# A fused attention read and MoE on one core: the whole program in another written order, some operations on other engines

## The chip, the cores and the metric

The kernel runs on one core of a Trainium2 chip. What counts is the device time of one execution in microseconds (us). The compute engines are TensorE (PE in the profile, its weight loads PEld), VectorE (DVE), ScalarE (ACT) and GpSimd (POOL); SyncE (SP) issues nearly all DMA transfers. About 0.5% of the time is what a measurement of this kernel can tell from no change.

## What is computed

Two stages, all in fp32. For each of 8 batches and 8 heads, x (512 by 64) reads from a state (32 by 64) and the state reads from x; the 544 rows of a batch, its heads side by side, are tokens of a feed-forward layer with squared ReLU:

```python
scores = scale * np.matmul(x, state.transpose(0, 1, 3, 2))
...
a /= a.sum(-1, keepdims=True) + 1e-09
xread = np.matmul(a, state)
scores2 = scale * np.matmul(state, x.transpose(0, 1, 3, 2))
...
sread = np.matmul(a2, x)
return np.concatenate([xread, sread], axis=2)
...
h = np.maximum(x @ w_in, 0.0)
return (h * h @ w_out).astype(np.float32)
```

There are 4352 tokens of 512 features, w_in is 512 by 2048 and w_out 2048 by 512. The weights come as 64-bit floats and are turned to fp32 on the chip (a *decode*: a clamp, an activation, a shift and an "or" of 32-bit words).

## The kernel before

**Precision.** TensorE multiplies in a rounded fp32 format. To keep fp32's accuracy, an operand is split in a rounded high part and the rest (hi and lo); a product takes three matmuls: hi hi, hi lo, lo hi. So behind nearly each tile there is a cast on ScalarE (hi) and a subtraction (lo), which a key puts on POOL or VectorE.

**Blocks.** The MoE's tokens come in nine blocks: 0 to 7 are the 512 read rows of a batch, 8 holds the 256 state rows of all batches. The read itself is not computed for blocks 0 to 7: the states are multiplied into w_in first (the tiles w2ps and w4ps), and the softmax's weights, transposed (k_hi, k_lo), are multiplied with that. For a block there are 16 pieces of the hidden layer. `hidden(blk, fc)` (tile ph) is 12 matmuls of 512 columns into one of two PSUM buffers, then ReLU and square on ScalarE or VectorE (r, ph), the cast g_hi and the subtraction g_lo, after which the buffer is free; `accumulate(blk, fc)` (tiles acc) is 12 matmuls more into four PSUM buffers. Blocks 0 and 1 break their sum off at pieces 4 and 8, keep it (first, part) and add it at the end. Blocks 5 to 7 are *fast*: two pieces of the hidden layer at a time go through seven products of sums of their quarters (steps `fast.blk.p.h`, products m1 to m7). Their operands are made by small sums and splits, f_sum, d_sum and e_sum (tiles s), p_lo, f_lo and b_lo (tiles a_g_lo and b_g_lo), each on VectorE or POOL by a key; the sums of w_out that they need are made in the steps `sums.p` (tiles v, sv, both, first).

**Order.** The program is cut in steps, each a Python generator. `PLAN` (from line 25) is a list of 2835 entries written out by hand; each entry advances the step of that name to its next yield, so PLAN sets the order in which instructions are issued. The string that would loosen it, `LOOSE_FROM = "never"`, is no entry of PLAN. Therefore the helper `InOrder` around each engine (lines 407 to 421) keeps every instruction in the written order on its engine, all 645 us long; since it makes the call, nearly each row of the profile stands on its line, 417:

```python
op = call(*args, **kw)
if self.held:
    self.tc.keep_in_program_order(op)
```

SP's queue of transfers is in written order as well. An instruction that waits for a tile from another engine holds up all that is written behind it on its own engine.

**Engines.** `SECOND` (from line 368) lists, by kind of operation, the keys that take the second of two engines: `pick(key, a, b)` gives b for a listed key; `evac(key)` copies out of PSUM on VectorE if listed, otherwise on ScalarE; `split(..., key)` subtracts on VectorE if listed, otherwise on POOL; `decode` clamps on POOL if listed, otherwise on VectorE. ROWS, which is not touched, names the small tiled products that are issued as one row.

**The start.** x of batches 0 and 1 is loaded in four pieces (xn), transposed by TensorE (px) and copied (xT); the states are transposed (pd) and copied (sD); `scores.0` (st) is copied (`keep_s`, tile e), transposed (pst), and softmax.0 makes k_hi and k_lo. w_in is decoded from wi_raw to wf; `direct_w2.0` makes its first product with the states (w2ps). 22 small matmuls of the identity (`warm`, tile pw) fill gaps. Then hidden.0.0 can begin.

**The end.** The last step, fast.7.7.1, has its products in the order m1, m4 and m3, m5 and m2, m7, m6, and `store_end` combines and writes the two last tiles.

Of the kernel before, what the change touches and what calls it, by code (L numbers as in the profile page):

```python
# [25 lines left out]
    ident warm.0 start.0 start.0 load.0.1 prep.0.0 warm.1 prep.0.0 warm.2 load_raw.0 load.0.1 load_states.0  # L26
        prep.0.1 load_states.0 load_states.0 prep.0.1 warm.3 decode_wi.0 neg_ident load_raw.1 warm.4 prep.0.0
        warm.5 start.1 warm.6 decode_wi.0 warm.7 prep.0.1 start.1 prep.0.0 load_wo.0 load.1.1 decode_wi.0
        decode_wi.0 states.0 warm.8 warm.9 prep.0.1 states.0 load_raw.2 decode_wi.0 scores.0 decode_wi.1 keep_s.0.1
        load.1.1 decode_wi.1 warm.10 keep_s.0.0 warm.11 prep.1.0 transposed_scores.0.1 decode_wi.1 prep_wo.0  # L30
        decode_wi.1 prep.1.0 transposed_scores.0.0 decode_wi.1 load_wo.1 direct_w2.0 softmax.0.1 direct_w2.0
        warm.12 softmax.0.1 direct_w2.0 softmax.0.1 warm.13 softmax.0.0 direct_w2.0 direct_w2.0 warm.14 softmax.0.0
        warm.15 direct_w2.0 softmax.0.0 warm.16 softmax.0.1 direct_w2.0 softmax.0.1 decode_wi.2 warm.17 second_w2.0
        softmax.0.0 softmax.0.0 prep_wo.1 prep_wo.0 prep_wo.0 warm.18 warm.19 second_w2.0 warm.20 second_w2.0
        warm.21 load_raw.3 prep.1.1 second_w2.0 second_w2.0 decode_wi.2 second_w2.0 prep.1.1 softmax.0.1 prep.1.1
        decode_wi.2 softmax.0.1 prep.1.0 load_wo.2 softmax.0.1 prep_wo.2 load_wo.8 decode_wi.2 prep.1.1 load_raw.4
        softmax.0.0 prep_wo.0 prep.1.0 load_wo.3 softmax.0.0 decode_wi.2 prep_wo.1 prep_wo.0 softmax.0.0 scores.1
        keep_s.1.0 decode_wi.3 load_states.2 keep_s.1.1 hidden.0.0 decode_wi.3 hidden.0.0 prep_wo.1 prep_wo.1
        hidden.0.0 decode_wi.3 prep_wo.0 hidden.0.0 transposed_scores.1.1 transposed_scores.1.0 decode_wi.4
        hidden.0.1 softmax.1.1 prep_wo.2 softmax.1.0 load_states.2 hidden.0.1 load_wo.4 softmax.1.1 prep_wo.3  # L40
        prep_wo.1 softmax.1.0 decode_wi.3 prep_wo.1 hidden.0.0 hidden.0.0 softmax.1.0 hidden.0.1 hidden.0.1
        accumulate.0.0 decode_wi.3 direct_w2.1 prep_wo.2 direct_w2.1 load_raw.5 accumulate.0.0 prep_wo.2
        direct_w2.1 direct_w2.1 direct_w2.1 decode_wi.4 direct_w2.1 direct_w2.1 softmax.1.1 hidden.0.1 load_wo.5
        second_w2.1 hidden.0.2 prep_wo.2 softmax.1.0 decode_wi.4 load_wo.7 hidden.0.1 accumulate.0.1 hidden.0.2
        hidden.0.2 decode_wi.4 softmax.1.0 load_raw.6 second_w2.1 second_w2.1 prep_wo.3 hidden.0.2 softmax.1.1
        hidden.0.3 softmax.1.0 accumulate.0.1 second_w2.1 decode_wi.4 prep_wo.2 hidden.0.3 softmax.1.0 exp_s.0.1
        hidden.0.2 hidden.0.2 softmax.1.1 second_w2.1 second_w2.1 load_wo.6 accumulate.0.2 hidden.0.3 exp_s.0.1
        prep_wo.3 softmax.1.1 decode_wi.5 decode_wi.5 prep_wo.3 softmax.1.1 softmax.1.0 hidden.0.3 load_states.2
        prep_wo.3 decode_wi.5 softmax.1.1 decode_wi.5 hidden.0.3 hidden.0.3 load_wo.11 decode_wi.5 prep_wo.4
# [1533 lines left out]
```

## Time and profile before

| | us |
|---|---|
| median of three runs | 644.88 (644.7 to 646.84) |
| the profiled execution | 646.96 |
| its span, first to last instruction | 645.1 |
| mean granted TensorE clock | 0.999 |

The profile is of one execution. A row of the timeline gives start, duration, engine, operation, the tile written and those read, and in brackets how long the engine had been idle before it and what released it. A row of the chain or of the waits has its columns named at the group. "x4" is the count of instructions taken together.

### The profile page before, as it was taken

How to read it: one execution, taken by the hardware profiler on the slowest of the kernel's cores; microseconds unless marked ns; L12 is line 12 of the kernel's file. 1: busy time of each engine (PE TensorE's matmuls, PEld its weight loads, DVE VectorE, ACT ScalarE, POOL GpSimd, SP SyncE). 2: the span in 40 equal slices, each digit the busy share in tenths (PEclk: the TensorE clock that was granted, in tenths of full speed). 3: DMA queues.
4: the chain of work that ended last, by engine and by line, in shares of the span. 5: the costliest groups of instructions: out<-in, count | busy, mean ns of one | idle time of the engine just before them, and what ended most of it. 6: DMA issues, size and time to landing. Idle time of an engine off the chain costs nothing.

```text
span 645.1 us, 12288 instructions
## 1 busy us (share of the span) xinstructions
PE 631.9 (98%) x4453; PEld 528.1 (82%) x4453; DVE 465.8 (72%) x927; ACT 394.7 (61%) x815; POOL 184.5 (29%) x172
## 2 busy tenths in 40 slices
PE   7999999999999999999999999999999999999996
PEld 6677787888777778777787788887999999999995
DVE  3999888675675688686958543579999866577637
ACT  3888667655654376655555542666877755565563
POOL 1665351201430124421023210223000344325451
PEclk9999999999999999999999999999999999999999
DMA  8888886989879889888977831421113332214202
GB/s 280 279 285 277 252 276 214 295 274 236 256 181 313 237 205 265 192 233 237 257 256 206 228 105 35 133 65 49 34 49 113 118 115 66 66 50 148 65 1 67
DMA packets 153132, 113.07 MB, mean 175 GB/s; under 512 B 93168, under 2 KB 126448, under 8 KB 153072
## 3 DMA queue, kind: packets, MB, share of 16 engines
q1 hardware_dynamic: 152784, 112.03, 59.5%
q8 instruction: 35, 0.57, 0.4%
q10 hardware_dynamic: 288, 0.26, 0.1%
q14 instruction: 25, 0.20, 0.1%
HBM read 72.94 MB, written 39.32 MB: 174 GB/s over the span
## 4 chain that ended last, share of the span: by engine, by line
PE 94%; DVE 2%; issue 1%; DMA 1%; ACT 1%; SPq 0%; POOLq 0%; POOL 0%; DVEq 0%; ACTq 0%
PE acc L417 37%; PE ph L417 30%; PE m L417 18%; PE w2ps L417 3%; PE w4ps L417 2%; PE pr L417 1%; PE st L417 1%; PE pw L417 1%; DMA xn<-in_x_dram 1%; PE px L417 1%; DVE g_lo L417 1%; DVE ph L417 0%; PE pst L417 0%; ACT r L417 0%; PE pa L417 0%
## 5 line engine op out<-in xcount | busy, mean ns | idle before, releaser
L417 PE MATMUL acc<-wo,g_hi 128*128 128x512 f32 x704 | 203.8, 393 | 0.0
L417 PE MATMUL ph<-k_hi,w 128*128 128x512 f32 x512 | 176.1, 392 | 0.4 <-DVE g_lo L417 0.3
L417 PEld LDWEIGHTS acc<-wo,g_hi 128*128 128x128 f32 x704 | 130.6, 188 | 32.6 <-issue 2.5
L417 ACT ACTIVATE r<-ph 128x512 f32<-128x512 f32 (+1 forms) x124 | 70.4, 569 | 97.8 <-PE ph L417 92.6
L417 PE MATMUL acc<-wo,g_lo 128*128 128x512 f32 x352 | 122.1, 391 | 0.0
L417 PEld LDWEIGHTS ph<-k_hi,w 128*128 128x128 f32 x512 | 96.2, 188 | 21.4 <-issue 1.2
L417 PE MATMUL ph<-k_lo,w 128*128 128x512 f32 x256 | 100.3, 392 | 0.0
L417 PEld LDWEIGHTS acc<-wo,g_lo 128*128 128x128 f32 x352 | 65.7, 188 | 14.7 <-DVE dec L417 0.4
L417 DVE TENSOR_TENSOR g_lo<-ph,g_hi 128x512 fp32r<-128x512 f32 (+1 forms) x95 | 60.4, 640 | 23.3 <-ACT g_hi L417 18.9
L417 DVE SCALAR_TENSOR_TENSOR ph<-ph,r 128x512 f32<-128x512 f32 (+1 forms) x48 | 31.1, 648 | 42.3 <-ACT r L417 42.1
L417 PEld LDWEIGHTS ph<-k_lo,w 128*128 128x128 f32 x256 | 48.2, 188 | 8.2
L417 POOL TENSOR_TENSOR w<-w_f,w 128x512 fp32r<-128x512 f32 x21 | 28.9, 1383 | 74.1 <-ACT w L417 37.9
L417 POOL TENSOR_TENSOR sp<-sp,m 128x512 f32<-128x512 f32 x25 | 26.6, 1067 | 72.3 <-DVE m L417 67.5
L417 ACT ACTIVATE g_hi<-r 128x512 fp32r<-128x512 f32 (+1 forms) x76 | 44.0, 582 | 4.9 <-PE acc L417 3.8
L417 POOL TENSOR_TENSOR wf<-wf,wf_hi 128x512 fp32r<-128x512 f32 x8 | 10.9, 1367 | 67.9 <-ACT wf_hi L417 67.9
L417 ACT ACTIVATE ph<-ph 128x512 f32<-128x512 f32 x40 | 23.5, 587 | 10.1 <-PE ph L417 8.6
L417 ACT CAST w<-w_f 128x512 fp32r<-128x512 f32 x40 | 24.2, 614 | 6.6 <-DMA w_f<-w_d 6.5
L417 POOL TENSOR_SCALAR dec<-wo_raw 128x512 f32<-128x512 f32 x10 | 20.5, 2051 | 13.3 <-DMA wo_raw<-in_moe_w_out_dram 13.1
L417 ACT ACTIVATE g<-r 128x512 f32<-128x512 f32 x35 | 21.8, 630 | 0.4
L417 DVE TENSOR_REDUCE m<-sp 128x16 f32<-128x512 f32 x28 | 18.7, 670 | 3.3 <-ACT sp L417 3.1
L417 POOL TENSOR_TENSOR s<-sf,s 128x512 fp32r<-128x512 f32 x6 | 7.8, 1292 | 43.3 <-ACT s L417 43.3
L417 ACT COPY w4o<-w4ps 128x512 f32<-128x512 f32 x16 | 9.1, 588 | 13.8 <-PE w4ps L417 9.7
(1072 smaller groups left out, 1309.6 us busy)
## 6 DMA issues: line engine op xcount, KB each, us to landing
w_f<-w_d SPq DMA_DIRECT2D x40, 256.0 KB, 4.0
wi_raw<-in_moe_w_in_dram SPq DMA_DIRECT2D x16, 512.0 KB, 5.1
wo_raw<-in_moe_w_out_dram SPq DMA_DIRECT2D x16, 512.0 KB, 5.7
xr<-in_x_dram SPq DMA_DIRECT2D x16, 512.0 KB, 5.5
wf<-win_f SPq DMA_DIRECT2D x16, 512.0 KB, 5.2
w_d<-w4o SPq DMA_DIRECT2D x32, 256.0 KB, 4.1
w<-w2a_d SPq DMA_DIRECT2D x16, 512.0 KB, 3.6
out_dram<-o SPq DMA_DIRECT2D x30, 256.0 KB, 3.0
```

The lines of the kernel that those rows point to most:

```text
L417: op = call(*args, **kw)
```

## The change

PLAN is written in another order, with the same 2835 entries, each as often as before; SECOND has other keys. No step, no instruction, no transfer and no buffer is added or taken away, and ROWS and all functions are as they were. On TensorE, 518 of 596 groups of matmuls keep their order among themselves; most others swap with a neighbour. 252 operations change their engine: 90 go from VectorE to POOL, 87 from POOL to VectorE, 39 from ScalarE to VectorE and 36 from VectorE to ScalarE. The first lines of PLAN, and some of SECOND:

```diff
 PLAN = """
-    ident warm.0 start.0 start.0 load.0.1 prep.0.0 warm.1 prep.0.0 warm.2 load_raw.0 load.0.1 load_states.0
-        prep.0.1 load_states.0 load_states.0 prep.0.1 warm.3 decode_wi.0 neg_ident load_raw.1 warm.4 prep.0.0
-        warm.5 start.1 warm.6 decode_wi.0 warm.7 prep.0.1 start.1 prep.0.0 load_wo.0 load.1.1 decode_wi.0
...
+    ident warm.0 warm.3 start.0 start.0 load.0.1 load.0.1 load_states.0 load_states.0 load_states.0 warm.18
+        load_raw.0 warm.21 warm.4 warm.2 warm.7 load_raw.1 start.1 start.1 prep.0.0 prep.0.0 prep.0.1 prep.0.0
+        prep.0.0 prep.0.1 prep.0.1 neg_ident decode_wi.0 prep.0.1 decode_wi.0 decode_wi.0 load_wo.0 prep_wo.0
...
 SECOND = """
-    b_lo: 5.6.1 6.0.0 6.1.1 6.4.1 6.5.0 7.0.0 7.0.1 7.1.0 7.4.1
-    d_sum: 5.6.1 6.0.0 6.0.1 6.3.1 7.1.0 7.1.1 7.2.1 7.4.1 7.5.0 7.5.1
-    decode_wi: 4 10 11 12 13
...
+    b_lo: 5.5.1 5.7.0 6.1.1 6.4.1 6.6.0 7.0.0 7.0.1 7.1.1 7.2.1 7.3.0 7.3.1 7.4.1 7.5.0 7.5.1
+    d_sum: 5.6.0 6.0.0 6.3.0 6.3.1 6.4.0 6.4.1 6.5.0 6.5.1 6.6.0 6.6.1 7.0.0 7.0.1 7.1.0 7.1.1 7.3.0 7.3.1 7.4.1
+        7.5.1 7.6.0 7.6.1
+    decode_wi: 2 6 11 14
...
-    sm_mul: 3.0
+    sm_mul: 0.0 0.1 2.0 3.0 4.1 6.0 6.1 7.0
...
```

What the order becomes at the places of which the prediction speaks, by the steps and the instructions they issue:

- Front: SP issues x of batch 0 in four pieces, three loads of the states, wi_raw0, wi_raw1, then x of batch 1 and wo_raw0; before, wi_raw0 stood between the pieces of x. Both multiplies of softmax.0 go from POOL to VectorE, decode_wi.2's clamp goes from VectorE to POOL, and decode_wi.3's "or" is written ahead of softmax.1's max and subtraction.
- Blocks 1 and 2: hidden.2.1's matmuls go ahead of the first part of accumulate.1.15; its g_lo goes ahead of the addition of block 1's first part.
- w4ps5 (later_w2.5) keeps hidden.2.5 as the neighbour ahead of it.
- read.3 is issued one accumulate earlier than the row "w2.2 scores.5", right ahead of which it was; transposes.1's four loads of eT come behind a load of wf.
- Block 8: the g_lo of pieces 13 and 14 are written ahead of operations of `sums`; the subtraction of a split weight (w2_lo 5.1) goes from VectorE to POOL.
- Blocks 5 to 7: of f_sum, d_sum, e_sum, p_lo, f_lo and b_lo, 5, 6 and 12 more are on POOL.
- End: d_sum, e_sum and f_lo of 7.6.1 go to POOL and f_lo of 7.7.1 to VectorE; m7 and m6 of 7.6.1 are issued behind m4, m3 and m5, m2 of 7.7.1.

## Rows read from the trace of the kernel before

**Rows 1.** The page: busy us (share of the span) and instructions of each engine

```profile
PE 631.9 (98%) x4453; PEld 528.1 (82%) x4453; DVE 465.8 (72%) x927; ACT 394.7 (61%) x815; POOL 184.5 (29%) x172
```

**Rows 2.** Windows: length, busy us of PE, PEld, DVE, ACT, POOL, clock, DMA share, GB/s

```profile
25.00:40.00 15.00, 14.30 (x98) 10.46 (x92) 14.47 (x25) 13.44 (x28) 11.67 (x8) 1.00 0.92 273
460.00:480.00 20.00, 20.00 (x136) 18.46 (x135) 19.42 (x49) 15.88 (x37) 0.00 (x0) 1.00 0.19 53
600.00:620.00 20.00, 20.00 (x139) 18.59 (x138) 10.70 (x20) 10.50 (x24) 10.40 (x15) 1.00 0.15 51
```

**Rows 3.** The chain that ended last, two pieces: start us, us, what

```profile
68.14 2.72 PE ph L417 x12
...
455.45 1.79 PE m L417 x15
```

**Rows 4.** TensorE's waits: who waited for whom, us in total, times, longest us

```profile
PE ph L417 <- DVE g_lo L417: 1.2, 3, 0.6
```

**Rows 5.** Timeline of the start

```profile
8.26 0.43 DVE L417 TENSOR_SCALAR wf<-wi_raw 128x512 f32<-128x512 f32 x1 [2.83 <-DMA wi_raw<-in_moe_w_in_dram]
...
13.23 1.09 PE L417 MATMUL st<-xT,sD 64*32 64x256 f32 x32
...
21.56 1.05 POOL L417 TENSOR_TENSOR sp<-sp,m 128x512 f32<-128x512 f32 x1 [0.46 <-DVE m L417]
...
22.19 0.59 ACT L417 CAST k_hi<-pa 128x512 fp32r<-128x512 f32 x1
...
25.08 0.49 PE L417 MATMUL ph<-k_hi,w 128*128 128x512 f32 x1
```

**Rows 6.** Timeline near 31 us

```profile
31.92 1.10 PE L417 MATMUL w2ps<-wf,sD 64*32 64x256 f32 x32 [0.63 <-DVE wf L417]
```

**Rows 7.** Timeline near 181 us

```profile
179.38 1.29 DVE L417 TENSOR_TENSOR o<-acc,part 128x512 f32<-128x512 f32 x2 [0.23 <-PE acc L417]
...
180.99 0.39 PE L417 MATMUL ph<-k_hi,w 128*128 128x512 f32 x1
181.71 0.50 PE L417 MATMUL ph<-k_hi,w 128*128 128x512 f32 x1 [0.33 <-DVE g_lo L417]
```

**Rows 8.** Timeline near 195 us

```profile
195.77 0.38 PE L417 MATMUL w4ps<-wf_hi,s 64*128 64x256 f32 x1 [1.05 <-DVE g_lo L417]
```

**Rows 9.** Timeline near 440 us

```profile
440.60 0.98 PE L417 MATMUL ph<-sr_k_hi,s 128*128 128x512 f32 x4 [0.23 <-DVE g_lo L417]
...
442.25 1.54 DVE L417 TENSOR_TENSOR w<-w_f,w 128x512 fp32r<-128x512 f32 x1 [0.17 <-ACT w L417]
...
444.27 0.94 PE L417 MATMUL ph<-sr_k_hi,s 128*128 128x512 f32 x4 [0.61 <-DVE g_lo L417]
```

**Rows 10.** Timeline of the end

```profile
630.33 0.42 DVE L417 TENSOR_TENSOR s7.6.1_7694<-g 128x256 f32<-128x256 f32 x1
...
634.45 1.16 DVE L417 TENSOR_TENSOR s7.7.1_7751<-g 128x256 f32<-128x256 f32 x2
...
636.29 0.51 PE L417 MATMUL m<-two_first,b_g_hi7.7.1_7769 128*128 128x256 f32 x2 [0.48 <-ACT b_g_hi7.7.1_7769 L417]
636.92 0.39 PE L417 MATMUL m<-two_first,b_g_lo7.7.1_7770 128*128 128x256 f32 x1
```

**Rows 11.** Groups of instructions: line, operation, count; busy us, mean ns; idle before

```profile
L417 DVE TENSOR_TENSOR w<-w_f,w 128x512 fp32r<-128x512 f32 x19 | 14.2, 745 | 1.1 <-ACT w L417 1.1
...
L417 POOL TENSOR_TENSOR w<-w_f,w 128x512 fp32r<-128x512 f32 x21 | 28.9, 1383 | 74.1 <-ACT w L417 37.9 <-DVE turned L417 23.0 <-DMA w_d<-w4o 13.2
...
L417 POOL TENSOR_TENSOR s7.5.0_7528<-g 128x256 f32<-128x256 f32 x1 | 0.7, 740 | 0.0
```

**Rows 12.** Timeline behind a row of small tiled matmuls

```profile
241.19 0.73 PE L417 MATMUL acc<-wo,g_hi 128*128 128x512 f32 x2
```

**Rows 13.** Timeline of SP and PE around read.1

```profile
153.53 2.84 SPq L417 DMA_DIRECT2D eT<-e_d  x4
...
165.09 1.10 PE L417 MATMUL pr<-xr,eT 128*32 128x64 f32 x64
```

More of the change, by code (lines that the diff above doesn't have):

```diff
@@ L339 @@
         fast.7.7.1 fast.7.7.1 fast.7.7.1 fast.7.7.1 fast.7.7.1 fast.7.7.1 fast.7.7.1 fast.7.7.1 fast.7.7.1
+        fast.7.7.1
 """
@@ L368 @@
 SECOND = """
-    b_lo: 5.6.1 6.0.0 6.1.1 6.4.1 6.5.0 7.0.0 7.0.1 7.1.0 7.4.1
-    d_sum: 5.6.1 6.0.0 6.0.1 6.3.1 7.1.0 7.1.1 7.2.1 7.4.1 7.5.0 7.5.1
-    decode_wi: 4 10 11 12 13
-    decode_wo: 0 1 2 3 4 5 6 9 11 12
+    b_lo: 5.5.1 5.7.0 6.1.1 6.4.1 6.6.0 7.0.0 7.0.1 7.1.1 7.2.1 7.3.0 7.3.1 7.4.1 7.5.0 7.5.1
+    d_sum: 5.6.0 6.0.0 6.3.0 6.3.1 6.4.0 6.4.1 6.5.0 6.5.1 6.6.0 6.6.1 7.0.0 7.0.1 7.1.0 7.1.1 7.3.0 7.3.1 7.4.1
+        7.5.1 7.6.0 7.6.1
+    decode_wi: 2 6 11 14
+    decode_wo: 0 1 2 3 5 6 7 9 10
     eT: 2.1 4.1 6.0 7.1
-    e_sum: 6.0.0 6.0.1 6.3.0 6.5.0 6.5.1 6.7.1 7.0.0 7.2.1 7.3.1 7.4.0 7.4.1 7.5.0 7.5.1
-    f_lo: 5.7.0 5.7.1 6.0.0 6.0.1 6.1.0 6.3.0 6.3.1 6.6.0 6.6.1 6.7.1 7.1.0 7.3.1 7.4.0 7.5.0 7.5.1 7.6.0 7.7.1
-    f_sum: 5.6.0 6.2.1 6.4.0 6.4.1 6.5.0 7.2.0 7.2.1 7.3.0 7.4.1 7.6.0
-    first: 0.3 1.1 1.2
+    e_sum: 5.4.1 5.5.1 5.6.1 5.7.1 6.2.0 6.4.0 6.4.1 6.5.1 7.0.0 7.0.1 7.1.0 7.1.1 7.2.1 7.4.0 7.5.0 7.5.1 7.6.1
+    f_lo: 5.6.1 6.1.0 6.1.1 6.2.0 6.3.0 6.5.0 6.5.1 6.6.1 6.7.0 6.7.1 7.1.1 7.4.1 7.5.0 7.6.1
+    f_sum: 5.6.1 6.1.0 6.1.1 6.4.1 6.5.0 7.0.0 7.0.1 7.1.0 7.3.0 7.3.1 7.5.0 7.5.1
+    first: 0.0 0.1 1.1
     g_pe: 0.1
-    g_sq: 5.0 5.1 5.2 5.3 5.4 5.5 5.6 5.7 5.8 5.9 5.10 5.11 5.12 5.13 5.14 5.15 6.0 6.1 6.3 6.4 6.5 6.8 6.9 6.11
-        6.14 7.0 7.1 7.3 7.5 7.6 7.9 7.11 7.12 7.13 7.15
-    k_lo: 0.1 1.0 1.1 2.0 2.1 5.0 5.1 6.0 6.1 7.0 7.1
+    g_sq: 5.0 5.1 5.2 5.3 5.4 5.5 5.6 5.7 5.8 5.9 5.10 5.11 5.13 5.14 5.15 6.0 6.2 6.3 6.4 6.6 6.8 6.11 6.12
+        6.14 6.15 7.0 7.1 7.2 7.3 7.4 7.5 7.6 7.7 7.9 7.10 7.12
+    k_lo: 0.1 1.0 1.1 2.0 2.1 4.1 5.0 6.0 6.1 7.0 7.1
     keep_s: 0.1
-    out: 2.0 2.1 3.1 3.3 4.3 5.1 5.3 6.2 7.0 7.1 7.2
-    p_lo: 6.3.0 6.3.1 6.4.0 6.5.0 6.5.1 6.7.0 7.2.1 7.3.0 7.5.1 7.6.0
+    out: 2.2 2.3 3.1 3.2 3.3 4.1 4.2 5.1 5.3 6.2 7.0 7.1 7.2
+    p_lo: 5.6.1 6.0.0 6.0.1 6.1.1 6.2.0 6.3.0 6.3.1 6.4.1 6.7.1 7.0.0 7.0.1 7.2.1 7.3.1 7.4.0 7.4.1
     part: 0.1 0.3 1.0 1.3
@@ L387 @@
         exp_s.2.1
-    sm_mul: 3.0
-    sm_sub: 1.0 1.1 5.1 6.1
-    square: 0.0 0.1 0.2 0.3 0.4 0.5 0.6 0.11 0.12 1.0 1.1 1.2 1.3 1.4 1.5 1.11 1.12 1.13 1.14 1.15 2.1 2.3 2.10
-        2.11 2.12 2.14 2.15 3.0 3.1 3.2 3.4 3.7 3.8 3.9 3.11 3.12 3.14 3.15 4.5 4.9 5.1 5.2 5.3 5.4 5.7 5.9 5.10
-        5.11 5.13 5.14 5.15 6.0 6.1 6.3 6.4 6.6 6.7 6.9 6.12 6.15 7.0 7.3 7.6 7.10 7.12 7.14 8.0 8.1 8.5 8.6 8.9
-        8.13 8.14 8.15
-    sv: 1.2 2.0
-    sv_lo: 0.1 1.1 1.3 2.0 6.3
-    w2_lo: 0.6 0.7 1.5 1.6 2.3 2.5 2.6 3.5 3.7 4.0 4.2 4.7 5.1 5.2 5.3 5.4 5.5 5.6 5.7
-    w2_out: 2.4.1 3.4.0 4.0.1 5.0.1 5.4.0 6.2.0 6.4.1 7.4.1
-    w2_pe: 0.0.0 0.0.1 0.1.0 0.1.1
-    w4_out: 0.1 1.3 2.2 3.1 3.3 4.0 4.1 4.2 5.0 6.0 6.1 6.2 6.3 7.1 7.2 7.3
-    w_in_lo: 0.0 0.1 1.0 2.0 3.1 4.1 5.0 6.1 7.0 7.1
-    w_out_lo: 6 7 10 12 13 14 15
-    wf_lo: 1.0 1.1 2.1 3.1 4.0 6.0 6.1 7.1
-    xT: 0.0.0 0.0.1 1.1.0
+    sm_mul: 0.0 0.1 2.0 3.0 4.1 6.0 6.1 7.0
+    sm_sub: 1.0 1.1 4.0 6.1 7.0 7.1
+    square: 0.0 0.1 0.2 0.3 0.4 0.5 0.6 0.11 0.12 1.0 1.1 1.2 1.3 1.4 1.5 1.11 1.12 1.13 1.14 1.15 2.1 2.3 2.4
+        2.10 2.11 2.13 2.15 3.0 3.2 3.3 3.4 3.5 3.10 3.12 3.15 4.2 4.4 4.10 4.13 4.15 5.1 5.2 5.3 5.4 5.7 5.9
+        5.10 5.11 5.13 5.14 5.15 6.0 6.1 6.3 6.4 6.6 6.7 6.9 6.12 6.15 7.0 7.3 7.6 7.10 7.12 7.14 8.1 8.3 8.4
+        8.5 8.6 8.9 8.11 8.12 8.14 8.15
+    sv: 0.2
+    sv_lo: 0.0 0.3 1.1 1.3 3.3
+    w2_lo: 0.4 0.7 1.4 2.3 2.4 2.7 3.1 3.3 3.6 3.7 4.0 4.1 4.2 4.4 4.5 4.7 5.2 5.3 5.4 5.5 5.6 5.7
+    w2_out: 2.4.1 3.4.0 4.0.0 5.0.1 5.4.0 6.0.0 6.2.0 6.4.1 7.4.1
+    w2_pe: 0.0.0 0.0.1 0.1.0 0.1.1
+    w4_out: 0.0 0.3 1.0 2.1 3.0 3.1 3.3 4.0 4.1 4.3 5.0 5.1 5.2 6.2 7.0 7.1 7.2 7.3
+    w_in_lo: 0.0 0.1 2.0 3.0 4.1 5.0 6.0 6.1 7.0 7.1
+    w_out_lo: 0 1 3 4 5 6 9 10 11 12 13 15
+    wf_lo: 3.0 3.1 4.0 4.1 5.0 5.1 6.0 6.1
+    xT: 0.0.0 0.1.0 0.1.1 1.1.0
 """
```

620 lines of the change are left out of this document (310 added, 310 removed).

## The prediction

> **What bounds the kernel now.** I read the busy times first, then stretches of them, then TensorE's waits, then the timeline at each wait. TensorE is busy for 631.9 of 645.1 us; no other engine passes 72% [rows 1]. Such a share could still hide a slow TensorE or one that waits inside its busy time. It does neither where I looked: in two stretches of 20 us, one with VectorE full (19.42) and one with three engines half idle, TensorE works all 20.00 us at a granted clock of 1.00, the upper level of 2.4 GHz [rows 2]. Twelve 512-column matmuls take 2.72 us, so one comes every 0.227 us; fifteen 256-column ones take 1.79, so 0.119 each [rows 3]. The change removes no matmul: the time falls only where TensorE waits now.
>
> The list of TensorE's waits has g_lo in three places [rows 4]; the timeline shows each, and the others. It understates them: a single 512-column matmul is shown 0.39 us long, though the next can follow after 0.227 [rows 3, 7], so the real wait is the one shown plus 0.16. I take the same 0.16 for shorter ones. Past the first 25 us these waits are 0.79 at 31.9 [rows 6], 0.49 at 181.7 [rows 7], 1.21 at 195.8 [rows 8], 0.39 at 440.6 and 0.77 at 444.3 [rows 9]. At 636.3 it is 0.64, and 0.28 more behind it: the pair there and the next start lie 0.63 apart, where two matmuls take 0.24, and 0.11 of that I take as the slow start of a pair after a stop, as another pair shows it (0.73 where 0.39 and 0.227 are 0.62) [rows 3, 10, 12]. Together 4.6 us. That and the front is all that an order can win, and the forecast lies in this frame.
>
> **The sum's base.** The profiled execution took 646.96 us for a span of 645.1; 1.86 lies around it. It is 2.1 above the median of 644.88. The terms are differences, so I take them off the median; from the profiled execution's own time the result would be 2.1 higher. 0.5% is 3.2 us: faster means under 641.7, slower over 648.1.
>
> **Part 1, the start (up to 39 us).** SP now issues wi_raw0 and wo_raw0 among the four halves of x. VectorE clamps wi_raw0 at 8.26, scores.0 runs at 13.23, ScalarE casts k_hi at 22.19, hidden.0.0 begins at 25.08 [rows 5]. The change issues all of x and the states first, then wi_raw0 and wi_raw1. The last x no longer waits behind 512 KB of weights, so I put the scores near 11.5, some 1.7 earlier (an estimate from the queue's order). The price: wi_raw0 lands later, and I put its clamp near 9.8, still in time for the first w2 product. But the way on to hidden.0.0 is ScalarE's row of casts, 0.59 each like k_hi's [rows 5]; the change takes none away, so I let the row close up by one cast, 0.6. Softmax.0's two multiplies go from POOL (1.05 each [rows 5]) to VectorE, and decode_wi.2's clamp the other way; VectorE is busy for 14.47 of the 15 us from 25 on [rows 2], so what it takes over early it pays for there. The "or" that held up the product at 31.92 [rows 6] is written ahead of softmax.1's first operations, but the accumulate before that product stands closer to its hidden too; I count nothing on top. **-0.65**; bounds -1.7 (the whole lead is kept) and +0.5 (VectorE's full stretch ends later). I stay near the casts' end, since they stand between.
>
> **Part 2, 181 us.** ph2.3 waits here for the PSUM buffer of ph2.1, which is free once VectorE has done ph2.1's g_lo, and that comes behind two sums of the parts, 1.29 us [rows 7]. The change writes this g_lo ahead of a sum, and ph2.1 ahead of one more piece of an accumulate, so that 18 matmuls lie between ph2.1 and ph2.3 (18 x 0.227 = 4.1 us) where there are 10 now (2.3). The wait goes: **-0.5**. The sums and their stores are late next; nothing reads them.
>
> **Part 3, 195.8 us.** The w4ps product keeps its place right behind ph2.5, and waits for the same g_lo [rows 8]: **0**.
>
> **Part 4, 440 us.** Two hiddens of block 8 wait for g_lo [rows 9]. On VectorE weight sums are queued ahead of it, and a weight's split that takes 1.54 where 0.745 is its mean [rows 9, 11]. The change writes both g_lo ahead of the sums and gives that split to POOL. Both waits go: **-1.15**. The split costs 1.383 on POOL [rows 11]; block 5 needs its weight much later. If POOL were late there, the wait would come back at that block.
>
> **Part 5, the end.** The cast that m1 7.7.1 waits for needs VectorE's two sums, which end at 635.61 after 1.16 us; one such sum is 0.42 [rows 10]. The change gives 1.1 us of step 7.6.1's work to POOL, takes f_lo 7.7.1 off POOL, and puts m7 and m6 of 7.6.1 behind the first products of 7.7.1. **-0.9** of 0.92; the bounds are 0 (m1 7.7.1 comes earlier in the new order and waits the same) and -1.2 (VectorE's last store operations move up too).
>
> **Part 6, switches.** read.3 stands apart from the small tiled matmuls it was joined to. Behind such a row the first two accumulate matmuls take the 0.11 more of [rows 12]: **+0.1**.
>
> **Part 7, transfers.** All of them stay, in another order. The one set that I found far behind is transposes.1's four eT loads, moved past a load of wf: now issued at 153.5, for a product at 165.09 [rows 13]. Issued 4 us later, with 2.84 for the issue, they leave some 4.7 us to land: **0**.
>
> **Part 8, blocks 5 to 7.** 252 operations change engine: 90 from VectorE to POOL and 87 back, 39 from ScalarE to VectorE and 36 back. Totals hardly move, but the fast blocks give POOL 23 operations more, 18 of them in blocks 6 and 7; one takes 0.74 there and 0.42 on VectorE [rows 10, 11]. Their cover is slack on all three: VectorE 10.70, ScalarE 10.50, POOL 10.40 of 20 us, with TensorE never short [rows 2]. **0**; without that cover, rival 4.
>
> **Part 9, what I don't see.** The thinnest lead I found between a hidden and its accumulate falls from 4.52 to 2.71 us (acc0.2). Many neighbours are swapped, and some will be late by a little: **+0.6**, from 0 (none) to +4.6 (as much as the present order has).
>
> Sum: -0.65 - 0.5 - 1.15 - 0.9 + 0.1 + 0.6 = -2.5. 644.88 - 2.5 = **642.4**.
>
> **Rivals.** (1) *The traced waits go, the scores' lead holds, nothing new waits*: -1.7 - 0.5 - 1.15 - 1.2 + 0.1 = -4.45, **640.4**. For it: each wait has one visible cause, which the new order takes away. Against it: ScalarE's casts.
> (2) *New waits give it back*: four the size of now's, 2.5 us on top of the forecast, **644.9**. For it: the present order has 4.6 us of them among other engines that have slack. Against it: the leads I followed are over 2.7 us.
> (3) *The new order doesn't act.* Every row stands on line 417, the helper that pins each instruction to the written order, so no chance for this.
> (4) *POOL is late in blocks 6 and 7* (slower). An added operation costs 0.32 more there, and a VectorE operation beside POOL can lose 0.80 (1.54 against 0.745 [rows 9, 11]): 1.12 if a product waits for it. From six of the 18 on it decides: 642.4 + 6.7 = **649.1**. For it: the two sums that took 1.16 ran beside a POOL operation. Against it: the slack of [rows 2].
> The Trainium skill (GPSIMD Engine Reference, 4.1 Engine selection and 8. Key points) puts elementwise work on VectorE, as GpSimd is about twice as slow on two inputs and shares its SBUF interfaces with it. By that rule the time would be rival 4's. The trace agrees on the price (1383 against 745 ns [rows 11]) but shows POOL idle for half of that stretch [rows 2].
>
> **How the numbers follow.** Forecast 0.38, rival 1 0.33, rival 2 0.15, rival 4 0.14. Faster by over 0.5% is rival 1, 0.33; within 0.5% the forecast and rival 2, 0.53; slower rival 4, 0.14. The range starts at 639.8 (rival 1, and 0.6 of the wait at 31.9) and ends at 646.4 (rival 2, and 1.5 more of the unseen waits); outside lie rival 4 and some 0.06 of the tails. The forecast alone spans 641.2 to 643.6: from no new wait and 0.6 more at the start, to twice the new waits and 0.6 less.
>
> **What would show it.** Right, step by step: scores.0 near 11.5 and hidden.0.0 near 24.5; no wait for g_lo at 181, 440 and 444 and none for b_g_hi at the end; the wait of w4ps at 195 still there; POOL some 13 us (18 x 0.74) busier in blocks 6 and 7 with TensorE still full. Wrong: new waits of TensorE of over 2 us in sum, above all on POOL in blocks 6 and 7, or a start that is not earlier.

## The result, and the profile after

The changed kernel is slower: 649.58 us (median of 10 runs, 647.88 to 652.51) against 646.43 for the kernel before (10 runs, 644.4 to 647.43). The ratio is 1.0058, 95% interval 1.0039 to 1.0076: some 3.7 us lost by the ratio (3.1 by the medians) where 2.5 were forecast to be won. A repetition gave 1.0053 (1.0031 to 1.0075). The profiled execution took 649.82 us, its span 648.0.

First the page of the changed kernel, part 1, which answers to [rows 1]:

```profile
PE 632.8 (98%) x4453; PEld 526.7 (81%) x4453; DVE 471.4 (73%) x927; ACT 394.1 (61%) x812; POOL 179.7 (28%) x175
```

No engine's busy time moves by 6 us, and the shares say nothing of the loss. TensorE's waits behind the first 25 us (who waited for whom, us in total, times, longest) answer to [rows 4]:

```profile
PE w2ps L419 <- DVE g_lo L419: 1.4, 1, 1.4
PE w4ps L419 <- DVE g_lo L419: 1.0, 1, 1.0
PE pa L419 <- POOL sp L419: 0.6, 1, 0.6
PE ph L419 <- DVE k_lo L419: 0.5, 1, 0.5
PE m L419 <- ACT b_g_hi7.7.1_7750 L419: 0.4, 1, 0.4
PE ph L419 <- DVE w2o L419: 0.2, 1, 0.2
PE ph L419 <- DVE g_lo L419: 0.2, 1, 0.2
```

The three waits for g_lo of [rows 7, 9] and the one for wf of [rows 6] are gone, w4ps is still there, as forecast. New are a w2ps product waiting for g_lo, pa waiting for POOL, and a hidden waiting for k_lo. I set both profiled executions side by side by the matmuls already done (for each group of matmuls: its start in the changed kernel less the time at which the kernel before had done the same number of columns). The changed kernel is 0.2 us late when hidden.0.0 begins, 1.3 at 46 us, 2.1 at 113, 2.4 at 223, 5.0 at 255 and 5.3 at 381; then 4.4 at 445, 3.6 at 448, 4.1 at 639 and 3.4 behind m1. So it loses on three stretches, wins on one, and gains a little at the end. The 0.8 between 46 and 113 us come from a hidden that waits for w2o (0.5 at 83 us) and from eight accumulate matmuls behind a w2ps product that take 2.41 us instead of 2.11 (0.3 at 112); the other profiled executions with the new start lose the same 0.8 to 1.1 there.

Three views show the places. Timeline of TensorE at softmax.1, and of VectorE ahead of it:

```profile
42.78 0.66 PE L419 MATMUL pa<-ident,sp 128*128 128x128 f32 x4 [0.60 <-POOL sp L419]
...
45.76 0.50 PE L419 MATMUL ph<-k_lo,w 128*128 128x512 f32 x1 [0.47 <-DVE k_lo L419]
...
37.28 0.67 DVE L419 TENSOR_REDUCE m<-e 128x1 f32<-128x512 f32 x1
...
38.39 1.72 DVE L419 SCALAR_TENSOR_TENSOR wf<-wi_raw,wf 128x512 uint32<-128x512 uint32 x1
40.03 0.41 DVE L419 TENSOR_TENSOR w<-w2ps,w 128x256 fp32r<-128x256 f32 x1
40.37 0.67 DVE L419 TENSOR_REDUCE m<-sp 128x16 f32<-128x512 f32 x1
```

The sum of softmax.1.1 (m from sp, 40.37) stands behind exp_s.0.1's maximum (m from e) and decode_wi.4's "or" (1.72). In the kernel before, the same sum stands ahead of that maximum:

```profile
38.28 0.67 DVE L417 TENSOR_REDUCE m<-sp 128x16 f32<-128x512 f32 x1
...
39.42 0.63 DVE L417 TENSOR_REDUCE m<-e 128x1 f32<-128x512 f32 x1
```

POOL's multiply, pa1.1, k_hi and k_lo of block 1 follow late.

Timeline near 242 us, ScalarE and TensorE:

```profile
237.67 0.64 ACT L419 ACTIVATE g_hi<-r 128x512 fp32r<-128x512 f32 x1
240.53 1.14 ACT L419 CAST w<-w_f 128x512 fp32r<-128x512 f32 x2 [2.22 <-DMA w_f<-w_d]
241.57 0.59 ACT L419 ACTIVATE r<-ph 128x512 f32<-128x512 f32 x1
...
243.78 0.88 PE L419 MATMUL w2ps<-wf,sT 64*32 64x256 f32 x23 [1.45 <-DVE g_lo L419]
```

ScalarE stands idle for 2.22 us because the next instruction in its written order is the cast of a weight, w2_2.7, that has not landed; behind it waits hidden.2.12's ReLU, behind that its g_lo, and behind that TensorE. The weight itself is first read by hidden.2.14 at 252.83, 12 us later. Its load is the w_f transfer in SP's timeline, here and in the kernel before:

```profile
235.72 1.26 SPq L419 DMA_DIRECT2D xp<-in_x_dram  x2
237.08 0.58 SPq L419 DMA_DIRECT2D w_f<-w_d  x1
```

```profile
232.45 0.33 SPq L417 DMA_DIRECT2D w_f<-w_d  x1
```

It is issued at 237.08, behind two stores, the first of which waits for VectorE, and four small pieces of x; before, it was issued at 232.45, with TensorE 2.4 us ahead of its later self, so it is 2.2 us later in the work.

The windows of blocks 5 to 7 (columns as in [rows 2]), before and after:

```profile
455.00:575.00 120.00, 120.00 (x834) 112.21 (x834) 94.11 (x217) 80.28 (x179) 28.77 (x37) 1.00 0.25 80
575.00:640.00 65.00, 64.19 (x447) 59.60 (x445) 44.59 (x94) 38.00 (x83) 25.80 (x35) 1.00 0.18 59
```

```profile
455.00:575.00 120.00, 120.00 (x820) 111.56 (x819) 95.40 (x212) 82.75 (x183) 40.33 (x46) 1.00 0.26 80
575.00:640.00 65.00, 64.56 (x454) 60.28 (x453) 38.13 (x78) 38.18 (x82) 36.14 (x47) 1.00 0.18 58
```

POOL is 22 us busier (54.6 to 76.5 in both windows) and TensorE is full all the same: rival 4 isn't what happened.

### The profile page after: what moved, and what is told of

It is laid out like the page before. It is cut to its first block, busy times and chain, and to the rows that moved or that the text cites. A ratio compares the mean times of both kernels' runs of the same rounds, so it can differ in the third digit from the quotient of the medians.

```text
span 648.0 us, 12269 instructions
## 1 busy us (share of the span) xinstructions
PE 632.8 (98%) x4453; PEld 526.7 (81%) x4453; DVE 471.4 (73%) x927; ACT 394.1 (61%) x812; POOL 179.7 (28%) x175
## 4 chain that ended last, share of the span: by engine, by line
PE 86%; DVE 5%; DMA 3%; ACT 2%; issue 2%; SPq 1%; POOLq 0%; DVEq 0%; POOL 0%; ACTq 0%
PE acc L419 34%; PE ph L419 28%; PE m L419 17%; PE w4ps L419 2%; PE w2ps L419 2%; DMA wi_raw<-in_moe_w_in_dram 2%; DVE wf L419 1%; PE pr L419 1%; SPq L419 1%; DMA w_f<-w_d 1%; PE st L419 1%; DVE g_lo L419 1%; DVE m L419 1%; ACT w L419 0%; ACT r L419 0%
## 5 line engine op out<-in xcount | busy, mean ns | idle before, releaser
L419 POOL TENSOR_TENSOR w<-w_f,w 128x512 fp32r<-128x512 f32 x18 | 23.9, 1330 | 91.9 <-ACT w L419 91.9
L419 POOL TENSOR_TENSOR sp<-sp,m 128x512 f32<-128x512 f32 x16 | 16.8, 1051 | 48.0 <-DVE m L419 42.2
L419 DVE COPY w4o<-w4ps 128x512 f32<-128x512 f32 x18 | 11.6, 683 | 10.7 <-PE w4ps L419 8.3
```

## Experiments

Each ratio is to the kernel before, run on the same chip; the changed kernel stands at 1.0058. Where a run tells by its trace, that is one execution. Edits are shown as moves in PLAN, with the place from the neighbouring entries.

| run | median us | ratio to before (95%) |
|---|---|---|
| load_early | 649.60 | 1.0046 (1.0030 to 1.0062) |
| three_loads_early | 648.00 | 1.0026 (1.0010 to 1.0043) |
| softmax1_early | 648.19 | 1.0030 (1.0010 to 1.0051) |
| loads_and_softmax1 | 648.33 | 1.0031 (1.0016 to 1.0046) |
| start_states_first | 650.71 | 1.0062 (1.0039 to 1.0084) |
| fast_keys_old | 652.18 | 1.0092 (1.0068 to 1.0117) |
| before_loads_late | 651.16 | 1.0073 (1.0045 to 1.0100) |
| before_181_and_440 | 648.56 | 1.0020 (1.0004 to 1.0036) |
| old_head_new_tail | 645.13 | 0.9979 (0.9962 to 0.9996) |
| new_head_old_tail | 650.78 | 1.0068 (1.0048 to 1.0089) |
| old_start_new_rest | 647.27 | 1.0020 (1.0005 to 1.0036) |
| fill_the_gap | 650.27 | 1.0074 (1.0051 to 1.0097) |
| all_repairs | 649.62 | 1.0050 (1.0031 to 1.0070) |
| changed_again | 649.62 | 1.0053 (1.0031 to 1.0075) |
| raw0_first | 648.49 | 1.0045 (1.0025 to 1.0064) |
| raw0_first_repairs | 647.33 | 1.0027 (1.0009 to 1.0045) |

### Which third of the program loses

Three grafts split the change in time. The written order and the engines of one kernel hold up to a step, those of the other from there on (entries already used left out).

```diff
 old_head_new_tail:  before | accumulate.8.3 (418 us) | changed
 new_head_old_tail: changed | accumulate.8.3 (418 us) | before
 old_start_new_rest: before | hidden.0.12 (114 us)    | changed
```

> The order and the engines of the kernel before up to accumulate.8.3 (about 418 us), those of the changed kernel from there on. Theory (the new order loses at its start and at late weight loads, and wins at 440 us; the end is a small gain): 0.5 + 0.87 off at 440 to 448, 0.2 to 0.8 off at the end, so 1.4 to 2.2 us under the kernel before, 644.3 to 645.1: faster than both. Rival (POOL's extra work in blocks 5 to 7 costs, and the first part of the program hides it): no faster than before, 646 or more.

> The other half: the changed order and engines up to accumulate.8.3, those of the kernel before from there on. If the parts add up as the theory has it, what the tail wins is lost: 5 us over before (the 5.0 us by which the profiled executions lie apart at 415 us), 650.5 to 652. Rival (POOL in the tail costs): faster than the changed kernel, under 649.

> The order and engines of the kernel before up to hidden.0.12 (about 114 us), those of the changed kernel from there on. Theory: the start and softmax.1 (with two small waits at 83 and 112 us) make 1.4 to 2.1 us of the loss and the loads at 200 to 270 us the rest, so 1.4 to 2.1 us faster than the changed kernel, 647.5 to 648.2. Rival (whatever is won before 120 us is taken back where the program waits for its weight loads, whose landing does not move with it): within 0.7 us of 649.6.

All three came within or close to what the theory gave (old_head_new_tail and old_start_new_rest just outside). The old head with the new tail is faster than both kernels: 645.13, 0.9979, so the new tail wins 1.4 us, and the run turned round loses 4.4 (1.0068). With the old start, 1.0020: of the 3.7 us, 2.5 lie ahead of 114 us, 2.7 between 114 and 418 (1.3 left over before, plus the 1.4 that the tail wins), and -1.4 behind. This is by the middles of the intervals. Each ratio is good to about 1.2 us, a difference of two to some 1.6; by new_head_old_tail the new tail wins 0.6 (1.0068 against 1.0058) instead of 1.4.

### The middle: weight loads

```diff
 load_early:          three_loads_early, also:
 start.5 start.5       load.3.1 hidden.2.3
+load_w2.2.7          +load_w2.2.3
 last_w2.1 last_w2.1   load.3.1 load.3.1 ...
 ...                   softmax.4.1
-load_w2.2.7          +load_w2.3.2
 last_w2.1             start.6
```

> The changed kernel with one entry moved: the load of weight w2_2.7 is issued ahead of last_w2.1's first store, so SP's queue no longer holds it behind a store that waits for VectorE and behind eight pieces of x. Theory (the transfer queue): ScalarE's 2.2 us wait for this weight ahead of hidden.2.12's ReLU goes, and with it TensorE's 1.4 us wait for g_lo at the w2ps product near 242; 1.9 to 2.7 us off the changed kernel's 649.6, so 647 to 647.7, and the stretch from 237 to 255 us as long as in the kernel before. Rival (POOL is late in blocks 5 to 7, or many small waits): the wait moves to a neighbour and less than 0.7 us is won.

> The changed kernel with the loads of three weights issued earlier: w2_2.3 ahead of six pieces of x and four stores, w2_2.7 ahead of last_w2.1's first store, w2_3.2 ahead of the eT loads. Theory (the new order issues weight loads so late that their landing, 2.8 to 6.2 us, decides whether ScalarE's cast, and what is queued behind it, holds TensorE up; where one such wait is gone the next takes its place): with all three early the waits at 202 to 206, 242 and 270 us go in every execution, 2 to 3 us off 649.6, so 646.6 to 647.6, and a narrower spread of times. Rival (each wait is of its own; the one load tried alone won nothing): less than 0.7 us. Second rival (x's pieces, now later, become the late ones): a new wait of VectorE's transposes on x, no gain.

One load alone won 0.8 us by the ratios, which the intervals don't tell from nothing; the rival seemed right. But its trace shows the wait at 242 us gone and another one 40 us earlier, at w2_2.3, which had cost nothing in the first execution. ScalarE, TensorE and the windows around it (length, TensorE's busy time and matmuls, granted clock, DMA share, GB/s), load_early:

```profile
201.61 0.62 ACT L417 CAST w<-w_f 128x512 fp32r<-128x512 f32 x1 [6.58 <-DMA w_f<-w_d]
202.13 0.58 ACT L417 COPY w4o<-w4ps 128x512 f32<-128x512 f32 x1
...
202.76 0.50 PE L417 MATMUL ph<-k_hi,w 128*128 128x512 f32 x1 [2.82 <-ACT w4o L417]
203.10 0.39 PE L417 MATMUL ph<-k_lo,w 128*128 128x512 f32 x1
203.33 0.98 PE L417 MATMUL ph<-k_hi,w 128*128 128x512 f32 x2
```

```profile
200.00:203.00 3.00, 0.23 (x1) 1.00 0.91 292
203.00:207.00 4.00, 4.00 (x12) 0.57 0.79 230
207.00:211.00 4.00, 4.00 (x19) 1.00 0.91 216
```

The load of w2_2.3 took 5.6 us from issue to landing here, 2.8 in the changed kernel's first profiled execution and 6.2 in that of start_states_first; the next entry of SP's queue is 512 KB of x. So the wait comes and goes with the execution: of ten profiled ones with w2_2.3 in its late place, TensorE waits for w4o, the copy behind that cast, in seven (0.65 to 3.23 us); of nine with w2_2.7 in its late place, it waits at 242 us in two (1.45 and 1.29). And a long one costs more than it lasts: after 2.82 us without work, the granted clock is 0.57 for 4 us, that is largely at the lower of its two levels, and the twelve matmuls of ph2.4 and ph2.6 after it need 4.46 us (202.76 to 207.22) instead of the 2.72 of [rows 3] (six each: a hidden of blocks 0 to 7 has 6 matmuls, not the 12 given in the section on the kernel before).

With all three loads early the kernel came to 1.0026, 2.1 us better than the changed one (good to some 1.6), inside the expected 2 to 3. In none of the four profiled executions with them early does TensorE wait at 202 or 242 us, nor, behind the start, for x. But something else on the chain is late then, in three_loads_early the low part of w2_2.7 itself, which VectorE makes behind other work:

```profile
252.91 0.65 DVE L417 TENSOR_TENSOR w<-w_f,w 128x512 fp32r<-128x512 f32 x1
...
253.62 0.74 PE L417 MATMUL ph<-k_hi,w 128*128 128x512 f32 x2 [1.31 <-DVE w L417]
```

With 0.80 more for a g_lo at 224 us, this execution (649.91, its run's median is 648.00) was no faster than the changed kernel's 649.82. So the 2.1 rests on the times; the traces show the two waits gone, and others in part in their place.

The other way round, the two loads put late in the kernel before, and nothing else:

```diff
 before_loads_late:
-load_w2.2.3                         -load_w2.2.7
 accumulate.2.0 ...                   last_w2.1 ...
 later_w2.4                          +load_w2.2.7
+load_w2.2.3                          load.5.1
 hidden.2.5
```

> The kernel before with two loads issued late and nothing else changed: w2_2.3 behind later_w2.4's stores, w2_2.7 behind last_w2.1's stores. Theory (loads): ScalarE waits for w2_2.3 near 195 and for w2_2.7 near 236, ahead of a copy and a ReLU, and TensorE with it: 1.5 to 4 us slower than before, 647.7 to 650.2. Rival (other parts of the new order make the loss): within 0.7 us of before.

It lost 4.7 us, more than the bound of 4. Its waits and the windows at the w2ps product:

```profile
238.94 1.14 ACT L415 CAST w<-w_f 128x512 fp32r<-128x512 f32 x2 [3.48 <-DMA w_f<-w_d]
...
242.53 1.53 PE L415 MATMUL w2ps<-wf,sT 64*32 64x256 f32 x23 [2.53 <-DVE g_lo L415]
```

```profile
240.00:242.50 2.50, 0.00 (x1) 0.00 (x0) 0.69 (x1) 1.77 (x5) 2.34 (x3) 1.00 0.92 235
242.50:246.10 3.60, 3.57 (x47) 1.14 (x47) 2.81 (x8) 2.29 (x4) 0.93 (x1) 0.53 1.06 270
```

The wait of 2.53 us is again followed by a stretch at 0.53, in which the 23 small matmuls take 1.53 where the changed kernel, after 1.45 us of waiting, needs 0.88. That is what my expectation lacked. In the old order, late loads on SP are thus enough to make a loss of this size.

### The start

```diff
 softmax1_early:                     start_states_first:
+softmax.1.1 softmax.1.1 softmax.1.1  neg_ident
 exp_s.0.1 second_w2.1 ...           +prep.0.1 states.0 states.0 scores.0 keep_s.0.0
 decode_wi.4                         +keep_s.0.1 transposed_scores.0.1 transposed_scores.0.0
 ...                                  decode_wi.0
-softmax.1.1                          ...
                                     +load.1.1 load.1.1
                                      decode_wi.0
```

> The changed kernel with softmax.1.1's exponential, sum and multiply written ahead of exp_s.0.1's maximum and decode_wi.4's or. Theory (VectorE's order at 37 to 42 us makes block 1's k_hi and k_lo late): TensorE's waits of 0.77 at pa1.1 (41.8) and 0.63 at hidden.1.0's k_lo (44.9) go, 1.0 to 1.4 us off, 648.2 to 648.6. Rival (VectorE is full there whatever the order): what is put behind becomes late, a wait of the same size for a w2 product or a g_lo, less than 0.4 us won.

> The changed kernel with its start written as the prediction took it to be: the last copy of x, the states, scores.0, keep_s and transposed_scores ahead of decode_wi.0, and x of batch 1 loaded ahead of the stores of the decoded weights. Theory A (the scores wait for sD, which ScalarE copies only behind its first decode, which waits for wi_raw0 to land): scores.0 near 9.3 instead of 11.8, but ScalarE's casts of the first w2 products still set hidden.0.0, which begins 0.3 to 1.0 us earlier than 25.0. Theory B (the scores are what holds the start up): hidden.0.0 begins 2 us or more earlier. Rival C (transfers set it): hidden.0.0 does not move by over 0.2 us. In all, 0 to 1 us off 649.6.

softmax.1 early gave 1.0030, 1.8 us better by the ratios, good to about 1.8 (1.4 by the medians): the theory, nearly as sized; in the trace the changed kernel's lead lost between 38 and 46 us comes back (0.9 late to 0.6 early against it). start_states_first won nothing. The scores moved to 8.77, but hidden.0.0 began at 25.92, later than in either kernel: TensorE's timeline shows what it then waited for:

```profile
8.77 1.10 PE L417 MATMUL st<-xT,sD 64*32 64x256 f32 x32 [0.68 <-ACT sD L417]
...
15.49 1.10 PE L417 MATMUL w2ps<-wf,sD 64*32 64x256 f32 x32 [2.56 <-DVE wf L417]
```

The first w2 product, not the scores, is the way to hidden.0.0, and it needs wf, decoded from wi_raw0 and wi_raw1; the new start issues both behind x and the states. Of the theories B falls and A's small gain didn't come. C (transfers) fits the first w2 product, at 15.49 against 15.52 in the changed kernel; hidden.0.0 came 0.9 later, with the granted clock at 0.68 and 0.50 between 16 and 20 us.

The chains of the first 30 us (start us, us, what) say the same. In the changed kernel the chain comes from wi_raw0 over VectorE's decode and softmax.0 to ScalarE's exponential (sp), ahead of the first cast of the product (w); in the kernel before, from x, and the cast follows the product at once:

```profile
4.28 5.91 DMA wi_raw<-in_moe_w_in_dram
...
16.02 0.70 DVE sp L419
...
16.75 0.63 ACT sp L419
17.38 0.27 ACT w L419
```

```profile
1.72 5.11 DMA xn<-in_x_dram
...
16.27 1.12 PE w2ps L417 x32
...
17.42 0.38 ACT w L417
```

Two more edits ask what else the start costs:

```diff
 fill_the_gap:                        raw0_first:
 warm.17                              load.0.1
+warm.21 warm.4 warm.2 warm.7        +load_raw.0
+warm.5 warm.12                       load.0.1
 scores.0
```

> The changed kernel with six of its small matmuls of the identity (four from the very front, two from later) moved into the gap ahead of scores.0; nothing else. Theory (the idle gap of 3.3 us lets the granted clock fall in many executions, and the start then ends up to 1.8 us later): clock 1.00 from 8 to 25 us, w2ps0 at 15.6 or earlier, 0.5 to 1.3 us off the changed kernel's 649.6 and 1.0058, so 1.004 to 1.005 of before. Rival (the low clock at the start is a matter of the execution, not of the gap): a clock under 0.95 between 8 and 25 us in spite of the fill, or no gain.

> The changed kernel with one entry moved: wi_raw0 is loaded ahead of the last piece of batch 0's x, as before the change. Theory (the landing of wi_raw0 sets the new start, since sD's copy and the decodes are queued behind it): it lands near 8.3, scores.0 begins near 10, hidden.0.0 at 23.1 to 23.9, and 0.7 to 1.4 us come off 1.0058, so 1.0035 to 1.0047 of before. Rival (the start is not held by this load): hidden.0.0 stays at 24.8 or later.

In fill_the_gap's profile the granted clock doesn't fall, but nothing is won (1.0074): its small matmuls use the PSUM buffers in which pd waits for ScalarE, so they wait for sD too, the scores start at 13.40 and hidden.0.0 at 25.77. In raw0_first VectorE's clamp of wi_raw0 begins at 8.69, but x's last piece now comes behind that load: TensorE stands 1.96 us for it, the scores begin at 12.09, and hidden.0.0 at 26.42, as the rival had it, in an execution whose clock was low; its 1.0045 is not told apart from 1.0058. Its windows:

```profile
8.00:16.00 8.00, 6.31 (x54) 4.81 (x55) 4.25 (x8) 2.87 (x7) 1.72 (x1) 0.57 0.92 317
```

In 8 of the 13 profiled executions with the new start, or an edit of it, the clock between 8 and 25 us is below 0.95, in none of 5 with the old one. In ten of the 13 TensorE stands idle for 2.0 to 3.9 us at a stretch ahead of the first w2 product, in no other execution for over 1.6, and the eight are among the ten. A 1.00 of these early windows is no proof of the upper level: in all_repairs, by its window at 1.00, scores.0 takes 1.96 us where 1.10 is its time, as in the executions whose clock was low.

The profiled executions also tell what the start costs. In the eight whose start is that of the changed kernel up to hidden.0.0, scores.0 begins 1.61 us behind VectorE's clamp of wi_raw0, which itself begins anywhere from 8.90 to 11.15; the first w2 product follows 3.7 us later in the two without a fall of the clock and 4.5 to 5.6 in the six with one; hidden.0.0 begins another 9.1 to 9.5 us later, in the mean at 25.3. In the five with the old start that last stretch is 8.9, and hidden.0.0 begins at 24.9. By the count of matmuls done, the six of the eight that keep softmax.1 as the change has it are 0.3 us later than the five at 40 us, 1.5 at 46 and 2.4 at 113, which is the 2.5 of old_start_new_rest: the falls of the clock and the row of casts take back the earlier scores and 0.3 more, softmax.1 makes 1.2, and the waits at 83 and 112 us the rest.

### Do the causes add up

loads_and_softmax1 joins three_loads_early and softmax1_early; raw0_first_repairs adds raw0_first to these, all_repairs adds fill_the_gap.

> The same three loads early, and softmax.1.1 early as well. Theory (two separate losses, one at 41 to 45 us on VectorE's order, one at 200 to 270 us on the loads): the gains add, 1.4 + 2 to 3 us off, 645.2 to 646.2: the kernel before or better. Rival (time won at 42 us is lost at the loads, which keep their own pace): no faster than three_loads_early by over 0.5 us.

> The changed kernel with the gap filled, softmax.1 early and the three loads early. Theory (three separate losses): 1.4 for softmax.1, about 2.1 for the loads and 0.5 to 1.3 for the clock come off 3.75 over before, so 0.9985 to 1.000 of before. Rival (the gains overlap, as loads_and_softmax1 had it): 1.002 or more.

> The same, with softmax.1 and the three loads early. Theory (three separate losses: the landing of wi_raw0, VectorE's order at softmax.1, the late loads): 0.998 to 1.001 of before. Rival (the gains overlap): 1.002 or more.

> The changed kernel itself, once more. Theory: its ratio to before comes out at 1.004 to 1.0075 again; its profiled execution may show the low clock between 8 and 25 us (it did in about six of nine executions of this start) and w2ps0 near 17, or the full clock and 15.5; near 202 and 242 us waits of TensorE of 1 to 5 us in sum.

They don't add up. loads_and_softmax1 (1.0031) is no faster than three_loads_early (1.0026), and all_repairs (1.0050) and raw0_first_repairs (1.0027) lie over the 1.002 of the rival, the last with an interval that reaches 1.0009, just inside the theory. In the profiled execution of loads_and_softmax1 the stretch from hidden.0.0 to 255 us is 2.6 us shorter than in the changed kernel's, less than the 3.5 of the sum (pa1.0 now waits 0.77), and its start was 1.8 us late at the first w2 product (granted clock 0.68 between 8 and 16 us); in raw0_first_repairs the same stretch is 2.8 us shorter, and the span is 644.5. But single executions differ by nearly as much: in changed_again, which has no edit, it is 2.2 us shorter, with no wait at 242 us and 0.68 at 201.5, less than was expected of it. How much of the gains overlaps stays open.

### Parts that the prediction priced

```diff
 before_181_and_440:                  fast_keys_old (changed order, old keys of
+hidden.2.1                           f_sum, d_sum, e_sum, f_lo, b_lo, p_lo):
 accumulate.1.15 ...                 -d_sum: 5.6.0 6.0.0 6.3.0 ...
+hidden.2.1 hidden.2.1               +d_sum: 5.6.1 6.0.0 6.0.1 ...
 accumulate.1.15                      ...
 ...
+hidden.8.14 x5
 sums.1 sums.1 sums.1
+hidden.8.13
 sums.1
+hidden.8.14
 sums.1
+hidden.8.13 x5
 sums.2 ...
+hidden.8.13
 sums.2
-w2_lo: ... 5.1 ...
+w2_lo: ...
```

> The kernel before with only two of the change's parts: hidden.2.1 ahead of accumulate.1.15 and its g_lo ahead of the additions (181 us), and block 8's g_lo of pieces 13 and 14 ahead of the weight sums with the split w2_5.1 on POOL (440 us). Theory (the prediction's parts 2 and 4 were right as sized): 0.49 + 1.15 = 1.6 us off 646.2, so 644.6. Rival (what is written behind becomes late): the waits move by a few us, less than 0.6 us off.

> The changed kernel with the old engines for f_sum, d_sum, e_sum, f_lo, b_lo and p_lo of blocks 5 to 7, so that POOL gets its 23 operations fewer again; the order is the new one. Theory (POOL's extra work in blocks 5 to 7 is hidden, TensorE is full there): within 0.5 us of 649.6, less than 0.5 us changes between 460 and 630 us. Rival 4 of the prediction (POOL late): 2 us or more faster. It can also be slower by up to 1 us where VectorE gets work in a place that the new order had left to POOL.

Both missed. In before_181_and_440, ph2.3 starts 0.60 us earlier than in the kernel before (0.10 of it from before the edit's place), as priced, but 5 us later 0.08 is left: accumulate.2.0, right behind ph2.3, waits for g_lo of hidden.2.0. In the changed kernel it is the same:

```profile
184.83 0.73 PE L419 MATMUL acc<-wo,g_hi 128*128 128x512 f32 x2
185.69 0.50 PE L419 MATMUL acc<-wo,g_lo 128*128 128x512 f32 x1
```

The second one comes 0.86 behind the first, where two matmuls and the slow start of [rows 12] are 0.56, and VectorE's g_lo ends at 185.64. At 440 us my own order was worse than the change's: block 8's work was ahead of the sums, but accumulate.8.12 waited 2.17 us for ScalarE's g_hi at 447.53, and the clock was then down to 0.62. So this run says nothing on part 4; the changed kernel's own trace does, and old_head_new_tail.

fast_keys_old is 2.2 us slower than the changed kernel (good to about 2), not the same: with the old keys, m1 7.7.1 waits 1.0 instead of 0.4 and a product of 7.5.1 0.3 for VectorE's b_lo, which is part of the 2.8 us that its profiled execution loses behind 448 us. The order and the keys of the last blocks belong together; POOL isn't late there, it takes work that VectorE would be late with.

## Why the prediction was wrong

The forecast was 642.4 and the range 639.8 to 646.4; the result, 649.58, is near rival 4's time but not by its cause, so that nearness is luck. Of the 7.2 us between forecast and result, 1.5 is the base: 644.88 was the median of three executions, 646.43 that of ten. The rest is the change.

- **The bound** was right: TensorE decides, and its waits count. It isn't at 1.00 throughout: behind long waits the granted clock fell, a price that the sum doesn't have. Nothing here contradicts that the waits of now are "all that an order can win".
- **Part 9 (+0.6)** was too small. That the new waits were bounded by +4.6 was in the text; behind 25 us the trace has 2.9 us of new ones.
- **Part 1 (-0.65) failed most**, and its bound of +0.5 as well: the run with the old start says +2.5. Its two times came right: the clamp at 10.21 and scores.0 at 11.82, in the mean of the eight executions 9.9 and 11.6, where 9.8 and 11.5 were put. What broke is the way on. "wi_raw0 lands later ... still in time for the first w2 product": the chain now comes from wi_raw0, and of the scores' 1.4 us the product keeps 0.7. "I let the row close up by one cast, 0.6": it opened by 0.3 to 0.6, since ScalarE's first cast stands behind softmax.0's exponential, which waits for VectorE; hidden.0.0 begins at 25.02 instead of 25.08. The fall of the clock had no term. And softmax.1.1's sum, behind other work on VectorE, lost 1.2 to 1.4 more, the waits at 83 and 112 us 0.8. I had counted VectorE's full stretch, but not which operation in it came last.
- **Part 2 (-0.5)** took the wait away and nothing from the time: I looked at the two hiddens that share a buffer, not at the accumulate behind them.
- **Part 3 (0)** was right: w4ps waits 1.0 as in [rows 8].
- **Part 4 (-1.15)** was right and a bit small: from 420 to 448 us the changed kernel comes 1.4 us closer (5.0 late to 3.6), and hidden.8.12 and 8.15 wait for nothing.
- **Part 5 (-0.9)**: m1 7.7.1 comes earlier and waits (0.35, against 0.48 in [rows 10]), 0.5 lost, then 0.7 won: -0.2 at TensorE, and 0.5 more won behind its last matmul. The whole tail, 4, 5 and 8 together, is -1.4 by old_head_new_tail, where I had -2.05.
- **Part 6 (+0.1)** is told by no run.
- **Part 7 (0) failed, too.** I looked for the transfer that was moved furthest, found eT, and left the rest at nothing. The loads of w2_2.3, w2_2.7 and w2_3.2 were moved by a few places in SP's queue, behind stores that wait. A cast of a late weight stops all that is written behind it on ScalarE. The middle stretch lost 2.7 us, and three entries moved back won 2.1 by the times.
- **Part 8 (0)** was right, and **rival 4** wrong: POOL is 22 us busier in blocks 5 to 7 (the 13 forecast were for 6 and 7 alone), and TensorE doesn't wait for it. The Trainium skill (GPSIMD Engine Reference, 4.1 Engine selection) puts a two-input elementwise operation on GpSimd at about twice VectorE's time; the trace agrees on that price (1383 against 745 ns [rows 11]), but the loss that the prediction tied to the rule did not come.
- **Rival 2** was the right kind, new waits that give it back, with a price too small by half: four waits "the size of now's". The waits on loads are larger than those on engines, since a landing varies by over 3 us, and in the middle of the program the four waits of 2.2 to 3.2 us were each followed by a stretch at a lower clock.

## What to carry to other kernels

When an order is compared, follow each load to its first reader, on the reader's engine: the cast of a weight that is needed late can stop a ReLU that is needed now, so the load's place in its queue, and what the entries ahead of it wait for, must be priced like a matmul. A wait that is removed is won only if nothing on the same chain comes due within the time won. Where a written order is changed as a whole, graft the halves of both: here the tail of one on the head of the other is the best of all (645.13, 0.9979).

## What the runs showed of the hardware

TensorE's granted clock fell after long waits in the middle of the program: after 3.23 us without work (start_states_first) it was 0.74 from 203 to 206 us and 0.77 from 206 to 210, after 2.82 us 0.57 over the next 4, after 2.53 us 0.53 over 3.6, after 2.17 us 0.78 and 0.62. After 1.72 us (fill_the_gap, ahead of 203.57) it didn't fall, and after the 1.45 us of the changed kernel at 243.78, 23 matmuls took 0.88 us, the full rate. In the start it fell in 8 of the 10 executions with a wait of 2.0 to 3.9 us; it didn't after the 3.34 us of the changed kernel and the 2.30 of load_early. The landing of one 256 KB load with the same neighbours in its queue took 2.8 to 6.2 us in ten executions, about 4.4 in the middle.
